# First pair transposed in two banks with half copies, a square moved to VectorE, and the second batch's loads moved behind its last transposes

## The chip, the cores and the metric

The kernel runs on one core of one Trainium2 chip. The time is the device time of that core in microseconds (us); each figure is a median of several executions unless it is said to be one. The engines are TensorE (PE; PEld is its weight load), VectorE (DVE), ScalarE (ACT), GpSimd (POOL) and SyncE (SP), which issues most transfers. The profile is that of one execution, and its span is about 1.8 us shorter than the time that is reported for the execution.

## The reference

Cosine attention on 8 batches of 12 heads, 448 positions and 64 columns, followed by an exact GELU layer:

```python
q_n = q / (np.linalg.norm(q, axis=-1, keepdims=True) + 1e-06)
k_n = k / (np.linalg.norm(k, axis=-1, keepdims=True) + 1e-06)
attn = softmax(np.matmul(q_n, k_n.transpose(0, 1, 3, 2)) / tau)      # tau = 0.1
x = np.matmul(attn, v).transpose(0, 2, 1, 3).reshape(3584, 768)      # shortened
h = x @ w_in                                                          # 768 x 2048
out = (0.5 * h * (1.0 + erf(h / sqrt(2)))) @ w_out                    # 2048 x 768
```

## The kernel before

Heads are worked on in pairs, six to a batch. For each pair: load q and k (`qk`), square, sum over 64 columns (`reduce`), take the root as exp(0.5 ln) on ScalarE, take the reciprocal (`rn`) and scale into bfloat16 (`qkb`) on GpSimd. The scaled pair is transposed (`qkT`). Then come four chunks of scores, an exponential for each (`pt`), and the products with ones (`sm`) and v (`o`). When six pairs are done, x of the batch goes through w_in (`hp`), GELU and w_out (`op`). The `op` matmuls of one batch fill TensorE in the attention of a later one. Batch 0 has nothing to fill with, so dummy matmuls (`spin`) keep TensorE busy.

The schedule is by hand: the order of the calls is the order on each engine. `upto(f, n)` calls f up to its n-th group, unless that has been done.

```python
    def mm_tile(name, shape=(128, 512), dtype=F32, aside=None):
        t = ps_mm.tile(list(shape), dtype, tag=f"mm{turn[0] ...}", name=name)   # (cut) two banks, in turn
    ...
    def square(g):
        ...
        elif g <= 3:
            nc.scalar.activation(sq, t, AF.Square)
        else:
            nc.gpsimd.tensor_tensor(sq, t, t, ALU.mult)
    ...
    def transposes(g):
        qkb = qkb_t.pop(g)
        qkT = qkTp.tile([128, 2, NC, CS], BF16, tag="qkT", name=f"qkT{g}")
        if g >= HP:                      # from batch 1 on: by a transfer
            nc.sync.dma_start_transpose(out=..., in_=...)      # (cut)
            return
        tp = mm_tile(f"tp{g}", (128, 2, NC, CS), BF16)
        for i in (1, 0):                 # k, then q
            for c in range(NC):
                nc.tensor.transpose(tp[:, i, c, :], qkb[:, i, c].rearrange("p h d -> p (h d)"), ident)
        nc.vector.tensor_copy(qkT, tp)
    ...
    def attention_first():               # batch 0
        for g in range(HP):
            scores(g, 0)                 # chunks 0 and 1
            if g == 0:
                roots(3)
                upto(scale, 3)
            if g < HP - 1:
                upto(transposes, g + 2)
            upto(reduce, min(g + 4, HP))
            if g in (3, 5):
                values(g - 3, 1, lambda: scores(g, 2))
            else:
                spin((4, 4, 1, 0, 1)[g])
                scores(g, 2)             # chunks 2 and 3
            ...
            spin((5, 5, 1, 2, 1, 2)[g])
    ...
    def attention(b, fill):              # batches 1 to 7, six pairs
        for i in range(HP):
            g = b * HP + i
            if i > 0:
                scores(g, 0)
            if i == HP - 1:
                roots(2 * b + 7)
            upto(scale, min(g + 4, nxt))
            upto(transposes, min(g + 4, nxt))
            upto(square, nxt + min(i, 3))
            run(plan[i][0])              # op matmuls of an earlier batch
            if i in (2, 4):
                both(g - 2, 0 if len(fill) % KF else 1)
            upto(reduce, nxt + min(max(i - 1, 0), 3))
            scores(g, 2)
            ...
            if b == 1 and i == 0:
                upto(load_qk, nxt + 4)
            ...
    ...
    upto(transposes, 1)                  # before batch 0
    spin(5)
    upto(reduce, 3)
```

Of the kernel before, what the change touches and what calls it, by code (L numbers as in the profile page):

```python
# [9 lines left out]
BF16 = mybir.dt.bfloat16  # L10
AF = mybir.ActivationFunctionType
ALU = mybir.AluOpType
# [3 lines left out]
def kernel(  # L16
# [17 lines left out]
    nc = tc.nc  # L34
    B, H, S, D = q.shape
    NC = 4
    CS = S // NC
# [51 lines left out]
    def mm_tile(name, shape=(128, 512), dtype=F32, aside=None):  # L89
        t = ps_mm.tile(list(shape), dtype, tag=f"mm{turn[0] if aside is None else turn[0] ^ aside}", name=name)  # L90
        if aside is None:
            turn[0] ^= 1
        return t
# [31 lines left out]
    def square(g):  # L125
        sq = sqp.tile([CS, 2, 2, NC, D], F32, tag="sq", name=f"sq{g}")
        sq_t[g] = sq
        t = qk_t[g]
        if g == 0:
            nc.scalar.activation(sq[:, 1], t[:, 1], AF.Square)  # L130
            nc.vector.tensor_tensor(sq[:, 0], t[:, 0], t[:, 0], ALU.mult)
        elif g <= 3:
            nc.scalar.activation(sq, t, AF.Square)
        else:
            nc.gpsimd.tensor_tensor(sq, t, t, ALU.mult)  # L135

# [42 lines left out]
# [3 lines that stand above are left out]
        qkT_t[g] = qkT  # L182
        if g >= HP:
            nc.sync.dma_start_transpose(out=qkT.rearrange("p i c s -> p (i c) s"),
                                        in_=qkb.rearrange("p i c h d -> p (i c h d)"))
            return
        tp = mm_tile(f"tp{g}", (128, 2, NC, CS), BF16)
        for i in (1, 0):
            for c in range(NC):
                nc.tensor.transpose(tp[:, i, c, :], qkb[:, i, c].rearrange("p h d -> p (h d)"), ident)  # L190
        nc.vector.tensor_copy(qkT, tp)


    def scores(g, c0):
        qkT = qkT_t[g]
        for c in (c0, c0 + 1):
            st = ps_st.tile([128, 2, 512], F32, tag="st", name=f"st{g}_{c}")
            for h in range(2):
                rows = slice(h * D, (h + 1) * D)
                nc.tensor.matmul(st[:CS, h, :S], lhsT=qkT[rows, 1, c, :], rhs=qkT[rows, 0, :, :],  # L200
                                 start=True, stop=True)
            pt = ptp.tile([CS, 2, S], BF16, tag="pt", name=f"pt{g}_{c}")
            nc.scalar.activation(pt, st[:CS, :, :S], AF.Exp, scale=inv_tau)  # L203
            pt_t[g, c] = pt
# [15 lines left out]
    def sums(g):  # L220
        sm = ps_acc.tile([128, 512], F32, tag="sm", name=f"sm{g}")
        columns(g, sm, lambda j, h, c: ones)
        tr = rcp.tile([128, S // 32, 32], F32, tag="tr", name=f"tr{g}")
        nc.vector.transpose(tr.rearrange("p b r -> p (b r)"), sm[:, :S])  # L224
        rc = rcp.tile([128, S // 32], F32, tag="rc", name=f"rc{g}")
        nc.vector.reciprocal(rc, tr[:, :, 0])
        rs = rcp.tile([128, S // 32, 32], F32, tag="rs", name=f"rs{g}")
        nc.vector.transpose(rs, rc.to_broadcast([128, S // 32, 32]))  # L228
        rs_t[g] = rs.rearrange("p b r -> p (b r)")

    def values(g, aside, between=None):
        b, p = divmod(g, HP)
        banks = [ps_acc.tile([128, 512], F32, tag="o", name=f"o{g}"), mm_tile(f"o{g + 1}", aside=aside)]
        for n, bank in enumerate(banks):
            if n == 1 and between:
                between()
            columns(g, bank, lambda j, h, c: v_t[g + j][:, h, c, n:D:2])
        for n in (1, 0):
            nc.vector.tensor_tensor(x_t[b][:, p + n, :], banks[n][:, :S], rs_t[g], ALU.mult)  # L239
        rs_t.pop(g)  # L240
        for j in range(2):
            v_t.pop(g + j)
            for c in range(NC):
                pt_t.pop((g + j, c))

    def both(g, aside):
        sums(g)
        values(g, aside)
# [55 lines left out]
    def upto(f, n, last=NG):  # L304
        while done.get(f, 0) < min(n, last):
            done[f] = done.get(f, 0) + 1
            f(done[f] - 1)

    def roots(n):
        upto(root, n, len(groups))  # L310


    def spin(n):
        ps = mm_tile("spin")
        for _ in range(n):
            nc.tensor.matmul(ps[:CS, :S], lhsT=ident, rhs=blank, start=True, stop=True)  # L316
# [3 lines left out]
    def attention_first():  # L320
        x_t[0] = xp.tile([128, HP, S], BF16, tag="x", name="x0")
        for g in range(HP):
            scores(g, 0)
            if g == 0:
                roots(3)
                upto(scale, 3)
            if g < HP - 1:
                upto(transposes, g + 2)
            upto(reduce, min(g + 4, HP))
            if g in (3, 5):  # L330
                values(g - 3, 1, lambda: scores(g, 2))
            else:
                spin((4, 4, 1, 0, 1)[g])
                scores(g, 2)
            if g in (2, 4):
                sums(g - 2)
            roots(min(g + 4, HP))
            upto(square, (5, 6, 6, 7, 8, 9)[g])
            upto(scale, min(g + 4, HP))
            upto(reduce, (0, 0, 0, 6, 7, 8)[g])  # L340
            upto(load_v, (2, 3, 3, 3, 3, 4)[g], NV)
            upto(load_wi, (1, 2, 3, 4, 4, 4)[g])
            upto(load_qk, (6, 6, 7, 8, 9, 12)[g])
            spin((5, 5, 1, 2, 1, 2)[g])
        upto(load_wo, 2)
        upto(reduce, HP + 3)
        both(HP - 2, 0)
# [3 lines left out]
    def attention(b, fill):  # L351
        fill = list(fill)
        plan = {96: ((20, 6), (8, 8), (0, 10), (8, 8), (0, 10), (8, 10)),
                128: ((24, 6), (13, 12), (0, 12), (12, 12), (0, 12), (12, 13))}[len(fill)]

        def run(n):
            for _ in range(n):
                fill.pop(0)()

        x_t[b] = xp.tile([128, HP, S], BF16, tag="x", name=f"x{b}")  # L360
        nxt = (b + 1) * HP
        for i in range(HP):
            g = b * HP + i
            if i > 0:
                scores(g, 0)

            if i == HP - 1:
                roots(2 * b + 7)
            upto(scale, min(g + 4, nxt))
            upto(transposes, min(g + 4, nxt))  # L370
            upto(square, nxt + min(i, 3))
            run(plan[i][0])
            if i in (2, 4):
                both(g - 2, 0 if len(fill) % KF else 1)
            upto(reduce, nxt + min(max(i - 1, 0), 3))
            scores(g, 2)
            if i in (0, 3):
                upto(load_v, g // 3 + 3, NV)
            if b == 1 and i == 0:
                upto(load_qk, nxt + 4)  # L380
            if i in (3, 4):
                upto(load_qk, nxt + i + 2)
            run(plan[i][1])
        both(nxt - 2, 1)


    def first(b):
# [24 lines left out]
        for n in range(nxt + 1, nxt + 4):  # L412
            upto(scale, n)
            upto(transposes, n)
        upto(load_qk, nxt + (10 if b else 7))
        upto(square, nxt + 6)
        upto(reduce, nxt + 6)
        for m in range(4):
# [13 lines left out]
    nc.scalar.preload_act_table_set(EXP_SET)  # L432
    upto(load_qk, 5)
    spin(24)

    late = nrm.tile([CS, 1], F32, tag="late", name="late", bufs=1)
# [6 lines left out]
    upto(scale, 1)  # L443
    upto(reduce, 2)
    roots(2)
    upto(square, 4)
    upto(scale, 2)
    upto(load_v, 2, NV)
    upto(load_wi, 1)
# [5 lines left out]
    for b in range(B):  # L455
        if b == 0:
            attention_first()
        else:
            attention(b, fill)
        first(b)  # L460
        sb, hf = divmod(b, 2)
        todo = [(t, ni) for t in (range(3) if hf == 0 else range(3, 7)) for ni in range(2)]
        if b == 0:
            todo.sort(key=lambda x: x[1])
        fill = [f for t, ni in todo for f in second_pieces(sb, t, ni)]
# [37 lines left out]
```

## Time and profile before

| What | Before |
|---|---|
| Time, the three runs known at first | 442.35 us (441.25 to 442.39) |
| Profiled span | 439.5 us |
| TensorE's share of the chain that ended last | 87% |
| First `hp` matmul of batch 0, of batch 1 | 37.79 us, 87.64 us |
| Dummy matmuls | 55, 15.7 us |

The start of batch 0's `hp` tells how long the start of the kernel took. The distance from there to batch 1's `hp` (87.64 - 37.79 = 49.85 us) tells what batch 0's second half and batch 1's attention took, whatever the start did. On TensorE's timeline of the kernel before (start, length, engine, line, operation) they are these lines:

```profile
37.79 18.50 PE L402 MATMUL hp<-x,wi 128*128 128x448 bf16 x96
...
87.64 18.34 PE L402 MATMUL hp<-x,wi 128*128 128x448 bf16 x96
```

The groups of GpSimd that the argument turns on are these, in the kernel before (line, engine, operation, count; busy us, mean ns of one; idle before it and what ended it):

```profile
L174 POOL TENSOR_TENSOR qkb<-qk,rn 112x512 bf16<-112x512 f32 x95 | 96.9, 1044 | 10.4 <-DVE rn L165 10.1
L135 POOL TENSOR_TENSOR sq<-qk 112x1024 f32<-112x1024 f32 x44 | 82.3, 1887 | 1.9 <-DMA qk<-in_k_dram 1.8
```

A pair's scaling is two GpSimd instructions of 1.04 us, and a square on GpSimd is 1.89 us.

### The profile page before, as it was taken

The page shows a single profiled execution, that of the slowest core. Times are in us where ns is not written, and L with a number is a line of the kernel's source. Part 1 is how long each engine was busy: PE and PEld are TensorE (multiplying, and loading weights), DVE is VectorE, ACT ScalarE, POOL GpSimd, SP SyncE. Part 2 cuts the span into 40 slices and gives each one's busy share as a digit, 9 for nine tenths or more (in the row PEclk, how much of TensorE's full clock was granted, in tenths as well). Part 3 has the DMA queues.
Part 4 walks back from the last instruction along what each step waited for, and adds up shares of the span by engine and source line. Part 5 has one row for each costly group of instructions (what it writes and reads, how often), then busy time and mean ns, then how long its engine had stood idle before and what let it go on. Part 6 is the DMA issues. An engine that isn't in the chain of part 4 may idle for free.

```text
span 439.5 us, 7942 instructions
## 1 busy us (share of the span) xinstructions
PE 428.5 (98%) x3303; PEld 215.6 (49%) x3303; DVE 163.1 (37%) x264; ACT 264.4 (60%) x381; POOL 203.3 (46%) x185
## 2 busy tenths in 40 slices
PE   8899999999999999999999999999999999999996
PEld 4444544455445554455444544445444554455563
DVE  4666315640355305451154501753045331341021
ACT  4995487746666467744767359655766457773300
POOL 3998848370935509291561906554190732300000
PEclk9999999999999999999999999999999999999999
DMA  9999999792683919775285843849077600911022
GB/s 216 247 239 208 184 200 232 177 202 51 109 168 84 202 22 122 162 128 139 30 151 140 160 107 53 180 115 204 1 130 152 131 5 1 131 38 35 1 72 73
DMA packets 83636, 54.99 MB, mean 125 GB/s; under 512 B 41872, under 2 KB 78608, under 8 KB 83600
## 3 DMA queue, kind: packets, MB, share of 16 engines
q1 hardware_dynamic: 66416, 42.35, 43.9%
q0 software_dynamic: 16784, 11.80, 19.5%
q8 instruction: 26, 0.43, 0.4%
q10 hardware_dynamic: 400, 0.33, 0.2%
q14 instruction: 10, 0.08, 0.1%
HBM read 45.61 MB, written 11.01 MB: 129 GB/s over the span
## 4 chain that ended last, share of the span: by engine, by line
PE 87%; ACT 6%; DMA 3%; POOL 2%; issue 1%; DVE 1%; POOLq 0%
PE hp L402 33%; PE op L263 31%; PE st L200 10%; PE o L217 8%; ACT pt L203 5%; PE sm L217 5%; DMA qkT<-qkb 2%; POOL qkb L174 2%; DMA qk<-in_q_dram 1%; PE spin L316 1%; POOL sq L135 0%; DVE nq L145 0%; ACT L426 0%; PE tp L190 0%; ACT lq L153 0%
## 5 line engine op out<-in xcount | busy, mean ns | idle before, releaser
L203 ACT ACTIVATE pt<-st 112x896 bf16<-112x896 f32 x192 | 164.3, 914 | 49.4 <-PE st L200 48.8
L263 PE MATMUL op<-wo,g 128*128 128x384 bf16 x896 | 158.0, 327 | 0.0
L402 PE MATMUL hp<-x,wi 128*128 128x448 bf16 x768 | 146.8, 353 | 0.0
L424 ACT ACTIVATE g<-hp 128x448 bf16<-128x448 f32 x128 | 66.9, 545 | 91.4 <-PE hp L402 91.1
L263 PEld LDWEIGHTS <-g 128*128 128x128 bf16 x896 | 81.9, 98 | 70.6 <-issue 21.6
L402 PEld LDWEIGHTS <-wi 128*128 128x128 bf16 x768 | 74.5, 98 | 71.8 <-issue 3.2
L174 POOL TENSOR_TENSOR qkb<-qk,rn 112x512 bf16<-112x512 f32 x95 | 96.9, 1044 | 10.4 <-DVE rn L165 10.1
L135 POOL TENSOR_TENSOR sq<-qk 112x1024 f32<-112x1024 f32 x44 | 82.3, 1887 | 1.9 <-DMA qk<-in_k_dram 1.8
L163 POOL TENSOR_SCALAR se<-sr 112x48 f32<-112x48 f32 x14 | 4.6, 326 | 156.9 <-ACT sr L162 156.9
L147 DVE TENSOR_REDUCE nq<-sq 112x16 f32<-112x1024 f32 x47 | 57.0, 1214 | 37.3 <-POOL sq L135 37.3
L200 PE MATMUL st<-qkT 64*112 64x448 bf16 x384 | 60.2, 373 | 4.1 <-ACT pt L203 2.9
L274 DVE COPY ot<-op 128x384 f32<-128x384 f32 x55 | 29.7, 541 | 75.8 <-PE op L263 75.8
L165 DVE RECIPROCAL rn<-se 112x48 f32<-112x48 f32 (+1 forms) x20 | 7.8, 392 | 104.2 <-POOL se L163 103.9
L217 PE MATMUL o<-pt,v 112*32 112x448 bf16 x768 | 40.9, 353 | 0.0
L200 PEld LDWEIGHTS <-qkT 64*112 64x112 bf16 x384 | 20.9, 124 | 40.1 <-issue 36.7
L239 DVE TENSOR_TENSOR x<-o,rs 128x448 bf16<-128x448 f32 x48 | 27.7, 619 | 5.0 <-PE o L217 2.3
L224 DVE STREAM_TRANSPOSE tr<-sm 128x448 f32<-128x448 f32 x24 | 15.6, 649 | 37.4 <-PE sm L217 37.3
L217 PEld LDWEIGHTS <-v 112*32 112x32 bf16 x768 | 20.1, 97 | 16.1 <-issue 0.7
L217 PE MATMUL sm<-pt,ones 112*32 112x448 bf16 x384 | 22.6, 355 | 0.0
L316 PE MATMUL spin<-blank,ident 112*112 112x448 bf16 x55 | 15.7, 425 | 1.5 <-POOL ident masks.py:199 1.3
L228 DVE STREAM_TRANSPOSE rs<-rc 128x448 f32<-128x448 f32 x24 | 15.5, 645 | 0.8
L120 POOL DMA_DIRECT2D v<-in_v_dram x17 | 14.0, 823 | 0.0
(33 smaller groups left out, 79.6 us busy)
## 6 DMA issues: line engine op xcount, KB each, us to landing
qk<-in_q_dram SPq DMA_DIRECT2D x48, 224.0 KB, 5.8
qk<-in_k_dram SPq DMA_DIRECT2D x47, 224.0 KB, 6.1
v<-in_v_dram POOLq DMA_DIRECT2D x15, 336.0 KB, 6.4
wi<-in_moe_w_in_dram POOLq DMA_DIRECT2D x4, 768.0 KB, 11.4
wo<-in_moe_w_out_dram POOLq DMA_DIRECT2D x4, 768.0 KB, 18.6
out_dram<-ot SPq DMA_DIRECT2D x7, 336.0 KB, 3.5
out_dram<-ot SPq DMA_DIRECT2D x8, 288.0 KB, 2.7
out_dram<-ot SPq DMA_DIRECT2D x8, 240.0 KB, 3.1
```

Of the source, the lines that this page charges most:

```text
L135: nc.gpsimd.tensor_tensor(sq, t, t, ALU.mult)
L147: nc.vector.tensor_reduce(nq, sq, mybir.AxisListType.X, ALU.add)
L174: eng.tensor_tensor(qkb[:, i].rearrange("p c h d -> p h c d"), t[:, i], rn[:, i].to_broadcast([CS, 2, NC, D]), ALU.mult)
L200: nc.tensor.matmul(st[:CS, h, :S], lhsT=qkT[rows, 1, c, :], rhs=qkT[rows, 0, :, :], start=True, stop=True)
L203: nc.scalar.activation(pt, st[:CS, :, :S], AF.Exp, scale=inv_tau)
L217: nc.tensor.matmul(bank[r:r + 32, :S], lhsT=weights(j, h, c), rhs=pt_t[g + j, c][:, h, :], start=(c == 0), stop=(c == NC - 1), tile_positi ...
L239: nc.vector.tensor_tensor(x_t[b][:, p + n, :], banks[n][:, :S], rs_t[g], ALU.mult)
L263: nc.tensor.matmul(ps[:, :NH], lhsT=g_t[sb][:, kf, t * 128:(t + 1) * 128], rhs=wo[:, kf, ni * NH:(ni + 1) * NH], start=(kf == 0), stop=(kf ...
L274: nc.vector.tensor_copy(ot[:, lo:hi], ps[:, :NH])
L316: nc.tensor.matmul(ps[:CS, :S], lhsT=ident, rhs=blank, start=True, stop=True)
L402: nc.tensor.matmul(hps[m], lhsT=wi[:, kd, m * 128:(m + 1) * 128], rhs=x_t[b][:, kd, :], start=(kd == order[0]), stop=(kd == order[-1]))
L424: nc.scalar.activation(g_t[sb][:, m, hf * S:(hf + 1) * S], hps.pop(m), AF.Gelu)
```

## The change

The intent: let the first scores start earlier by transposing and copying the first pair in halves; close ScalarE's 0.73 us gap by putting a third chunk of scores ahead of the next transposes; and take the wait of batch 1's fifth pair away by putting the squares and loads of the next batch behind the last transposing transfers.

```diff
         if g == 0: ...
-        elif g <= 3:
+        elif g <= 2:
             nc.scalar.activation(sq, t, AF.Square)
+        elif g == 3:
+            nc.vector.tensor_tensor(sq, t, t, ALU.mult)
 ...
         tp = mm_tile(f"tp{g}", (128, 2, NC, CS), BF16)
-        for i in (1, 0):
+        for i in range(2):
             for c in range(NC):
                 nc.tensor.transpose(...)
-        nc.vector.tensor_copy(qkT, tp)
+            if g == 0:
+                nc.vector.tensor_copy(qkT[:, i], tp[:, i])
+                tp = None if i else mm_tile("tp0b", (128, 2, NC, CS), BF16)
+        if g > 0:
+            nc.vector.tensor_copy(qkT, tp)
 ...
             if g == 0:
+                upto(square, 4)
+                upto(reduce, 4)
                 roots(3)
                 upto(scale, 3)
+                scores(g, 2, 1)
 ...
-                spin((4, 4, 1, 0, 1)[g])
-                scores(g, 2)
+                spin((0, 4, 1, 0, 1)[g])
+                scores(g, *((2, 2) if g else (3, 1)))
 ...
-            spin((5, 5, 1, 2, 1, 2)[g])
+            spin((4, 5, 1, 2, 1, 2)[g])
 ...   (attention of batch b)
+            late = 1 if b == 1 else 0
             if i == HP - 1:
+                upto(reduce, nxt + 3)
                 roots(2 * b + 7)
 ...
-            upto(square, nxt + min(i, 3))
+            upto(square, nxt + min(max(i - late, 0), 3))
 ...
-            upto(reduce, nxt + min(max(i - 1, 0), 3))
+            upto(reduce, nxt + min(max(i - 1 - late, 0), 3))
 ...
-            if b == 1 and i == 0:
+            if late and i == 2:
                 upto(load_qk, nxt + 4)
 ...   (before batch 0)
     roots(2)
-    upto(square, 4)
     upto(scale, 2)
```

## The prediction

> **What bounds the kernel now.** I read the page's totals and its chain first.
>
> ```profile
> PE 428.5 (98%) x3303; PEld 215.6 (49%) x3303; DVE 163.1 (37%) x264; ACT 264.4 (60%) x381; POOL 203.3 (46%) x185
> ...
> PE 87%; ACT 6%; DMA 3%; POOL 2%; issue 1%; DVE 1%; POOLq 0%
> ```
>
> TensorE carries 87% of the chain that ended last. Outside its own work there are only 13% of 439.5 us, most of it in the first 38 us (six pairs of heads of batch 0, where TensorE is kept busy with 55 dummy matmuls, 15.7 us, and waits on the exponentials). So a change of the first pair and of one load can only touch a few pieces. I then took the chain in order of time over the first 42 us:
>
> ```profile
> 7.81 1.53 POOL qkb L174
> 9.35 1.43 issue
> ...
> 10.80 2.05 POOL qkb L174 x2
> ...
> 14.60 1.72 ACT pt L203 x2
> ```
>
> Until 12.9 us the chain runs through GpSimd's scaling (qkb), then through TensorE to ScalarE's exponentials (pt). To see what each engine waits for I read the timelines of VectorE, ScalarE, GpSimd and TensorE (start, length, instruction, idle time before it):
>
> ```profile
> 10.64 0.56 DVE L191 COPY qkT<-tp 128x896 bf16<-128x896 bf16 x1
> 11.12 1.20 DVE L147 TENSOR_REDUCE nq<-sq 112x16 f32<-112x1024 f32 x1
> 13.90 0.19 DVE L158 TENSOR_REDUCE se<-root 112x16 f32<-112x32 f32 x1 [1.58 <-ACT root L157]
> 14.12 0.25 DVE L165 RECIPROCAL rn<-se 112x16 f32<-112x16 f32 x1
> ```
>
> ```profile
> 14.60 1.72 ACT L203 ACTIVATE pt<-st 112x896 bf16<-112x896 f32 x2 [0.73 <-PE st L200]
> ```
>
> ```profile
> 14.46 2.04 POOL L174 TENSOR_TENSOR qkb<-qk,rn 112x512 bf16<-112x512 f32 x2
> ```
>
> ```profile
> 9.80 1.11 PE L316 MATMUL spin<-blank,ident 112*112 112x448 bf16 x5
> 11.26 0.59 PE L200 MATMUL st<-qkT 64*112 64x448 bf16 x4 [0.34 <-DVE qkT L191]
> ```
>
> Three things matter. The first copy starts at 10.64 although its transposes ended at 9.97: VectorE does the reciprocal of pair 1 (10.47 to 10.72) just before it. ScalarE is idle 0.73 us before the exponential at 14.60. GpSimd starts pair 2's scaling at 14.46, as soon as its reciprocal (14.12) is there, and from then to 24.2 its timeline has no gap: scale 14.46, square 16.47, scale 18.32, square 20.32, scale 22.17.
>
> In batch 1 TensorE has one real gap:
>
> ```profile
> 73.75 1.47 PE L263 MATMUL op<-wo,g 128*128 128x384 bf16 x8
> 75.83 0.58 PE L200 MATMUL st<-qkT 64*112 64x448 bf16 x4 [0.61 <-DMA qkT<-qkb]
> ```
>
> ```profile
> 68.06 6.31 SPq L184 DMA_TRANSPOSE qkT<-qkb  x2
> ```
>
> The second transfer-transpose was issued at 68.06, after six loads (64.78 to 67.95), although its input was ready when GpSimd ended at 66.34. It landed 7.73 us later, 75.79.
>
> **What the Trainium skill says.** "VectorE: DVE Perf Modes", section "Why PSUM operands drop a tier": a PSUM operand caps a 16-bit copy at twofold rate. The trace agrees: 896 elements at 2 per 0.96 GHz cycle are 0.467 us, the copy took 0.56. So my estimate of a half copy is 448/1.92 = 0.233 plus the same 0.09, 0.33 us, 0.24 from start to start. Same page, "The TRN2 errata": an fp32 tensor_tensor takes (N+151)/0.96 ns. The trace agrees at N=512 (691 against 693 ns), so I estimate the square moved to VectorE, N=1024, at 1.22 us. "DMA: Bandwidth & Descriptors", section "Issuing engines are not separate DMA queues": transfers of all issuers share the 16 engines and interleave. This fits a transpose that took 7.7 us behind six loads against 2.9 us at best. "TensorE: Matmul & The Clock Gate", section "What's actually happening": the clock halves after an idle window of about 3.4 us. The granted clock was 1.00 in every stretch that I asked for, and no run here shows that limit yet.
>
> **The change, part by part, from the new order of instructions.** (1) Pair 0 transposes q first and k second, in two banks, with two half copies. The q transposes can now start when the earlier dummies end (9.09), k's at 9.40 as before. But VectorE's order is still reciprocal of pair 1, then the copies. They start at 10.64 as before and end near 11.2: 0.24 + 0.33 = 0.57 against 0.56. Gain: nothing.
>
> (2) The two banks alternate, and the five dummies after the transposes keep their turn: they now fall into the bank of the first half. The first dummy waits for the first half copy in the built program (before it waited only for TensorE itself). It starts near 11.02 instead of 9.80; five times 448 columns at 2.4 GHz, 0.187 us, make 0.93, so the first scores start near 11.95 instead of 11.26, and the first exponential near 12.4 instead of 11.70: +0.7 us.
>
> (3) The third score chunk comes before the next transposes and the four dummies go. It needs only the first exponential's buffer (free near 13.3), so the exponential of chunk 2 follows the root directly: 12.4 + 2 x 0.81 + 0.34 + 0.12 = 14.5, against 14.60. The 0.73 us gap pays for part (2).
>
> (4) Square 3 leaves ScalarE (1.06 us, beside other work) for VectorE, and its 1.22 + 1.20 us (square and reduce) are placed before pair 2's small reduce and reciprocal: 11.12 + 1.20 + 1.22 + 1.20 = 14.74. Part (2) alone puts the root at 14.6 too. So the reciprocal of pair 2 runs near 14.95 to 15.2 instead of 14.12 to 14.37, and GpSimd's scaling of pair 2 starts at 15.3 instead of 14.46: +0.83. GpSimd has no gap for 10 us after, so the delay stays. Pair 2's transposes move from 16.70 to 17.4; the dummies and the scores of pair 1's second half follow, from 17.96 to 18.65, and the exponential behind them goes from 18.40 to 19.1. From 22 us to the first hp matmul at 37.79 the chain is exponentials and TensorE without slack. I count +0.7 to +0.8 us, although the first exponentials are back in time.
>
> (5) In batch 1 squares and loads of the next batch come after the last transposes. The blocked transpose can be issued near 66.4, 1.7 earlier, with no load in front of it, and should land by 72 to 73, before it is needed at 75.2: -0.61. The loads come at about 70, land after 75, and the squares, 1.88 us each and serial on GpSimd with a v issue of 0.8 between, end near 81, the last reduce near 82. It is needed at 82.4 (logarithm at 83.03, less 0.6). Slack 0.4 us, so on average I count -0.5.
>
> Sum: 0.75 - 0.5 = +0.25 us, on 442.35.
>
> **Rivals.** A: the start gains, as intended. If the half copies and the dummy wait cost nothing, the first exponentials stay at 11.70 and the 0.73 gap goes: -0.7, with -0.6 from batch 1, 441.05. For it: the gap is real, and ScalarE is the chain there. Against it: GpSimd's timeline without a gap, and VectorE's order in (4), which holds even without (2). B: the later loads make the roots of the next batch late; ScalarE, in order, stops and batch 1 gives back its 0.6 or more: 443.1 with the rest as counted. For it: 0.4 us slack only, and the DMA engines at 90% busy or more in each slice from 60 to 66 us. Against: the queue has gaps from 78 on. C: with five dummies fewer (four before chunk 2, one after) and five others waiting, TensorE idles in about half of 9.8 to 15.7 us, its clock drops for some microseconds, and the start loses another 1.5: 444. For it: the clock halves on lack of activity, as the page says. Against it: no single idle stretch that I find is over 1.5 us, well under 3.4.
>
> **Range and chances.** Three quarters for my sum (442.6) and one quarter for A (441.05) give 442.2. The three runs of before differ by 1.1 us themselves (441.25 to 442.39), more than the effect; with B above and A below I take 440.8 to 443.4. Two per cent are 8.8 us; all parts together move less than 2, so "same" is 0.985.
>
> **What would show it.** Right: the first dummies after the transposes waiting for VectorE's copy near 11.0; first scores near 11.95; chunk 2's exponential near 14.5; GpSimd's third scaling near 15.3; first hp matmul near 38.5 instead of 37.79; no gap before the scores at 75.8; granted clock 1.00. Wrong: hp starting before 37.6 (A), ScalarE waiting for a late reduce near 83 us (B), a clock under 0.95 in 10 to 20 us (C).

## The result, and the profile after

The changed kernel took 442.77 us (median of 4 runs, 442.15 to 443.84), the kernel before 442.08 us beside it (441.25 to 442.39). The ratio is 1.0021, 95% interval 0.9996 to 1.0046. Ratios here are the mean time of one kernel's fast runs over that of the other's of the same rounds, so they are not quite the ratio of the quoted medians. The time is the same within 2%. The predicted 442.2 us was 0.6 us low, inside the range.

The profiled span is 440.8 us instead of 439.5. The page's totals of the changed kernel hardly move:

```profile
PE 427.9 (97%) x3298; PEld 215.4 (49%) x3298; DVE 164.8 (37%) x266; ACT 263.4 (60%) x380; POOL 203.3 (46%) x185
...
PE 87%; ACT 5%; DMA 3%; POOL 2%; issue 1%; DVE 1%; POOLq 0%
```

The timelines carry the reading. VectorE after the change:

```profile
10.41 0.33 DVE L194 COPY qkT<-tp 128x448 bf16<-128x448 bf16 x1
10.66 0.38 DVE L194 COPY qkT<-tp0b 128x448 bf16<-128x448 bf16 x1
...
12.08 1.62 DVE L135 TENSOR_TENSOR sq<-qk 112x1024 f32<-112x1024 f32 x1
...
15.08 0.25 DVE L167 RECIPROCAL rn<-se 112x16 f32<-112x16 f32 x1
```

ScalarE and GpSimd after the change:

```profile
12.27 1.72 ACT L209 ACTIVATE pt<-st 112x896 bf16<-112x896 f32 x2 [2.28 <-PE st L206]
...
14.34 1.71 ACT L209 ACTIVATE pt<-st 112x896 bf16<-112x896 f32 x2
```

```profile
10.57 2.04 POOL L176 TENSOR_TENSOR qkb<-qk,rn 112x512 bf16<-112x512 f32 x2 [1.40 <-DVE rn L167]
...
15.42 2.04 POOL L176 TENSOR_TENSOR qkb<-qk,rn 112x512 bf16<-112x512 f32 x2 [1.32 <-DVE rn L167]
```

TensorE after the change:

```profile
10.79 1.11 PE L324 MATMUL spin<-blank,ident 112*112 112x448 bf16 x5 [1.20 <-DVE qkT L194]
11.83 0.59 PE L206 MATMUL st<-qkT 64*112 64x448 bf16 x4
...
17.52 0.37 PE L192 MATMUL tp<-ident,qkb 112*128 112x112 bf16 x4 [0.64 <-POOL qkb L176]
...
38.49 18.50 PE L415 MATMUL hp<-x,wi 128*128 128x448 bf16 x96
...
73.17 0.59 PE L206 MATMUL st<-qkT 64*112 64x448 bf16 x4 [1.19 <-DMA qkT<-qkb]
...
88.92 18.33 PE L415 MATMUL hp<-x,wi 128*128 128x448 bf16 x96
```

The reader is to see three things. First, the dummies, which before waited only for their turn, now wait 1.20 us for a copy of VectorE. Second, pair 2's scaling starts at 15.42 (before 14.46), and batch 0's `hp` starts 0.70 us later. Third, the wait of batch 1's fifth pair is gone, but the fourth pair's scores wait 1.19 us for a transposing transfer. The distance between the two `hp` starts is 50.43 us, 0.58 more than before. 0.70 + 0.58 = 1.28 us, the whole difference of the two spans.

The 0.70 us hides something. Pair 1's scaling, which waits for the first loads and which the change does not touch, started at 10.57 us here. In the profile before it started at 10.80:

```profile
10.80 2.04 POOL L174 TENSOR_TENSOR qkb<-qk,rn 112x512 bf16<-112x512 f32 x2 [1.46 <-DVE rn L165]
```

So the start after the change was 0.23 us ahead because a load landed earlier. Counted from pair 1's scaling, `hp` began 26.99 us later before (37.79 - 10.80) and 27.92 us later after (38.49 - 10.57), and the start lost 0.93 us. I use this count wherever the loads of two executions differ.

The late transfer is the first one of the last three in batch 1, the one for the fourth pair. I call it T9. It was issued at 63.52 us before and at 64.22 after. Its landing, before and after, as us from the issue:

```profile
DMA to landing us min/median/max: 6.3/6.3/6.3
```

```profile
DMA to landing us min/median/max: 8.9/8.9/8.9
```

After the change T9 was needed 71.98 - 64.22 = 7.76 us after its issue. What the DMA engines moved from 60 to 80 us, in 40 slices of 0.5 us, before and after:

```profile
GB/s 191 192 190 186 194 217 278 302 259 131 178 165 177 156 169 186 271 250 254 260 268 262 289 258 262 281 246 192 62 136 283 287 293 285 346 277 204 123 154 157
```

```profile
GB/s 188 185 193 190 195 192 184 224 297 304 258 166 156 42 14 14 191 181 168 193 210 190 240 87 5 9 175 321 324 328 328 313 332 332 318 328 324 326 377 393
```

Both are busy, but after the change two stretches stand out in which almost nothing moved while T9 was under way: 42, 14 and 14 GB/s at 66.5 to 68.0 us, and 5 and 9 GB/s at 72 to 73 us. Before, no slice is under 62.

So the questions are: is it the start that costs 0.70 us (0.93 counted from pair 1's scaling), and which part of it? Is T9's lateness made by the later loads? And is +1.28 us of one pair of profiles what the change costs on average?

### The profile page after: what moved, and what is told of

Its sections match the earlier page's. It is cut to its first block, busy times and chain, and to the rows that moved or that the text cites. A ratio compares the mean times of both kernels' runs of the same rounds, so it can differ in the third digit from the quotient of the medians.

```text
span 440.8 us, 7935 instructions
## 1 busy us (share of the span) xinstructions
PE 427.9 (97%) x3298; PEld 215.4 (49%) x3298; DVE 164.8 (37%) x266; ACT 263.4 (60%) x380; POOL 203.3 (46%) x185
## 4 chain that ended last, share of the span: by engine, by line
PE 87%; ACT 5%; DMA 3%; POOL 2%; issue 1%; DVE 1%; POOLq 0%
PE hp L415 33%; PE op L269 31%; PE st L206 10%; PE o L223 8%; PE sm L223 5%; ACT pt L209 4%; DMA qkT<-qkb 2%; POOL qkb L176 2%; DMA qk<-in_q_dram 1%; PE spin L324 1%; DVE nq L147 0%; ACT L439 0%; PE tp L192 0%; POOL wi L298 0%; ACT lq L155 0%
## 5 line engine op out<-in xcount | busy, mean ns | idle before, releaser
L230 DVE STREAM_TRANSPOSE tr<-sm 128x448 f32<-128x448 f32 x24 | 15.6, 649 | 36.6 <-PE sm L223 36.6
L324 PE MATMUL spin<-blank,ident 112*112 112x448 bf16 x50 | 14.6, 434 | 2.5 <-POOL ident masks.py:199 1.3
```

What stands on the lines that cost most here:

```text
L324: nc.tensor.matmul(ps[:CS, :S], lhsT=ident, rhs=blank, start=True, stop=True)
```

## The experiments

Twelve kernels ran, in four calls. The kernel before, beside them, had medians of 441.63, 442.70, 442.19 and 441.68 us (11 runs each, 440.76 to 445.75). Four kernels separate the start from batch 1, then the pieces of the start. The letters in the expectations name theories made after the result. They are not the prediction's rivals: here A says that the later loads themselves make the fourth pair's scores wait, and B that the shifted start does. C says that two costs work side by side in the start, the waiting dummies and square 3 ahead of pair 2's reciprocal, and that GpSimd's row of scalings and squares, which follows, sets the end. F says that T9's landing is settled anew in each execution.

### The start alone

The changed kernel, with batch 1's order as before:

```diff
-            late = 1 if b == 1 else 0
-                upto(reduce, nxt + 3)
-            upto(square, nxt + min(max(i - late, 0), 3))
+            upto(square, nxt + min(i, 3))
-            upto(reduce, nxt + min(max(i - 1 - late, 0), 3))
+            upto(reduce, nxt + min(max(i - 1, 0), 3))
-            if late and i == 2:
+            if b == 1 and i == 0:
                 upto(load_qk, nxt + 4)
```

> The changed kernel with batch 1 as before (only the start is changed). Theory A (start and batch 1 lose independently): first hp matmul near 38.5 us, as in the changed kernel (before 37.79), and in batch 1 the gap of before (about 0.6 us, ahead of the scores of the fifth pair) and no gap ahead of the scores of the fourth pair; span near 440.2, ratio to before near 1.0016. Rival B (the batch 1 gap of 1.19 us comes from the start being 0.7 us late, so that the weight loads run into the first transposing transfer): the gap ahead of the fourth pair shows here too; span near 440.8 or more.

443.10 us (442.11 to 444.36, 6 runs), ratio 1.003 [1.0001, 1.0058]. TensorE's timeline:

```profile
38.51 18.50 PE L413 MATMUL hp<-x,wi 128*128 128x448 bf16 x96
...
76.71 0.59 PE L206 MATMUL st<-qkT 64*112 64x448 bf16 x4 [0.77 <-DMA qkT<-qkb]
```

The start costs 38.51 - 37.79 = 0.72 us without the rest of the change (27.92 - 26.99 = 0.93 us counted from pair 1's scaling, at 10.59). The old wait is back at the fifth pair, and the fourth pair has none (T9 landed after 6.1 us). That is against B. This is the only kernel whose interval lies above 1, one of ten intervals, and by little. It fits the loss that the trace shows for the start. Two of the six executions had a mean granted clock of 0.991 and 0.989. I come back to that.

### The later loads alone

The kernel before, with batch 1's part of the change only (the same five edits the other way):

```diff
+            late = 1 if b == 1 else 0
+                upto(reduce, nxt + 3)
-            upto(square, nxt + min(i, 3))
+            upto(square, nxt + min(max(i - late, 0), 3))
 ... (reduce and load_qk as in the change)
```

> The kernel before with only the batch 1 part of the change. Theory A: first hp matmul near 37.8; in batch 1 the transposing transfers follow each other with no loads behind the first, the fourth pair's scores wait about 1.2 us and the fifth pair's do not; span near 440.1, ratio near 1.0013. Rival B: with the start on time no gap ahead of the fourth pair, 0.6 us gained; span near 438.9, ratio near 0.9986.

442.02 us (440.50 to 442.33, 6 runs), ratio 0.9996 [0.9968, 1.0023].

```profile
37.64 18.50 PE L404 MATMUL hp<-x,wi 128*128 128x448 bf16 x96
...
86.81 18.33 PE L404 MATMUL hp<-x,wi 128*128 128x448 bf16 x96
```

The distance is 49.17 us, 0.68 less than before, and no pair waits; T9 landed after 6.9 us. The wait of 1.2 us that theory A expected for the fourth pair did not come. In this execution the later loads gave what the prediction counted.

### Dummies that wait for nothing

The changed kernel, but the five dummies write the bank of the sums, which is free then:

```diff
-    def spin(n):
+    def spin(n, free=False):
-        ps = mm_tile("spin")
+        ps = ps_acc.tile([128, 512], F32, tag="sm", name="spin") if free else mm_tile("spin")
 ...
-    spin(5)
+    spin(5, free=True)
```

> The changed kernel with the five dummies in the bank of the sums, so that they do not wait for the half copy. Theory C (two causes at the start in parallel: the waiting dummies, and square 3 with its reduce on VectorE ahead of pair 2's reciprocal): the first scores start near 11.0 instead of 11.83 and the first exponential near 11.5 instead of 12.27, but GpSimd's scaling of pair 2 still starts near 15.3 to 15.4 and the first hp matmul stays near 38.4 to 38.5. Rival D (the waiting dummies are the whole cause): scaling of pair 2 near 14.6 and first hp matmul near 37.7.

441.71 us (441.54 to 442.37, 4 runs), ratio 0.9997 [0.9959, 1.0034]. In the profiled execution a load of the first pairs landed late: pair 1's scaling began at 10.95 instead of 10.57, and everything behind it is shifted by 0.38 us.

```profile
11.46 0.59 PE L206 MATMUL st<-qkT 64*112 64x448 bf16 x4 [0.86 <-DVE qkT L194]
```

```profile
15.80 2.04 POOL L176 TENSOR_TENSOR qkb<-qk,rn 112x512 bf16<-112x512 f32 x2 [1.33 <-DVE rn L167]
```

The first scores came 0.37 us earlier in spite of the late load. Pair 2's scaling did not: 15.80 less 0.38 is 15.42, as in the changed kernel. Nor did `hp`, which began at 38.87: less 0.38 that is 38.49, again the same. The dummies' wait is real, but the end of the start does not hang on it here, and rival D, that it is the whole cause, falls. In batch 1 there was no wait, and the distance was 49.28 us.

### Both costs of the start taken back

As above, and square 3 with its reduce back where the kernel before had them. The half copies and the three chunks stay:

```diff
-        elif g <= 2:
+        elif g <= 3:
             nc.scalar.activation(sq, t, AF.Square)
-        elif g == 3:
-            nc.vector.tensor_tensor(sq, t, t, ALU.mult)
 ...
-                upto(square, 4)
-                upto(reduce, 4)
                 roots(3)
 ...
     roots(2)
+    upto(square, 4)
```

> The changed kernel with free dummies and with square 3 on ScalarE again, its reduce where it was before; half copies and three score chunks ahead stay. Theory C: GpSimd's scaling of pair 2 near 14.3 and the first hp matmul at 37.6 to 37.8, as before or 0.1 better, since GpSimd's work without a gap then sets it; no 0.7 us gain. Rival E (the half copies and chunks are worth the 0.73 us that ScalarE idled): first hp matmul near 37.1. The gap ahead of the fourth pair in batch 1 stays near 1.2 if it comes of the batch 1 part.

441.54 us (440.34 to 442.11, 4 runs), ratio 0.9986 [0.9953, 1.0019]. GpSimd and TensorE:

```profile
14.27 2.04 POOL L174 TENSOR_TENSOR qkb<-qk,rn 112x512 bf16<-112x512 f32 x2 [0.19 <-DVE rn L165]
16.27 1.88 POOL L135 TENSOR_TENSOR sq<-qk 112x1024 f32<-112x1024 f32 x1
```

```profile
37.66 18.50 PE L411 MATMUL hp<-x,wi 128*128 128x448 bf16 x96
...
72.40 0.58 PE L204 MATMUL st<-qkT 64*112 64x448 bf16 x4 [1.26 <-DMA qkT<-qkb]
```

Here the intent of the change was reached for the first pair: chunk 2's exponential started at 13.57, 1.03 us earlier than before, of which 0.25 is an earlier load (pair 1's scaling at 10.55). Counted from there, pair 2's scaling began after 3.72 us (before 3.66, changed kernel 4.85) and `hp` after 27.11 (before 26.99, changed kernel 27.92). So the loss of the start is back to 0.12 us, and the early exponential gained nothing: pair 2's transposes can't start before its scaling ends, at 16.31. That much of theory C holds. That the whole row of GpSimd sets the end is not shown: behind pair 2's scaling, the chain of the kernel before runs through TensorE and the exponentials. The granted clock in this execution was 0.85, 0.50 and 0.79 in 12 to 14, 14 to 16 and 16 to 18 us. By an estimate from the chain that hides about 0.2 us: the transposes began at 16.45, 0.1 after the scaling, and took 0.69 us instead of 0.57.

In batch 1 the fourth pair waited 1.26 us although the start was on time. So the shifted start is not what makes T9 late, and theory B falls for the second time. Nor is it the later loads alone, which had no wait in two of the four traces with them so far. T9's landing varies.

### The changed kernel again

One look at the unedited kernel, and the first run of the second call:

> The changed kernel, unedited, one more look. Theory F (whether the first transposing transfer of batch 1 lands late is settled anew in each execution): the start repeats (first hp matmul at 38.5, plus or minus 0.1 for the first load), but the gap ahead of the fourth pair's scores need not be 1.19 us again; two of four executions with the same batch 1 part had 1.2, two had none. Rival G (it belongs to this kernel's timing): 1.1 to 1.3 us again.

442.83 us, span 441.1, mean clock 0.991. TensorE:

```profile
40.02 18.50 PE L415 MATMUL hp<-x,wi 128*128 128x448 bf16 x96
...
89.19 18.33 PE L415 MATMUL hp<-x,wi 128*128 128x448 bf16 x96
```

The same program, nearly the same span, and quite other parts. The distance is 49.17 us with no wait in batch 1 (T9 landed after 6.8 us), and `hp` began 1.53 us later than in the first profile. So T9's landing is settled anew, as theory F says, but the start did not repeat as it expected. 0.41 of the 1.53 is a load that landed late (pair 1's scaling at 10.98). For the rest, look at two stretches (us from the start, length; busy us and count of PE, PEld, DVE, ACT, POOL; granted clock, DMA share, GB/s):

```profile
8.00:14.00 6.00, 3.11 (x22) 1.49 (x20) 5.00 (x8) 2.85 (x6) 4.25 (x5) 0.91 1.15 243
14.00:16.00 2.00, 2.00 (x13) 1.12 (x12) 1.93 (x5) 1.90 (x5) 0.67 (x2) 0.50 1.12 237
```

TensorE was busy for 3.11 of 6 us, and then its clock was 0.50, 0.50 and 0.56 to 20 us. The fall of the clock cost 1.53 - 0.41 = 1.12 us. In the first profile TensorE was busy 3.98 us in the same stretch and the clock was 1.00 throughout. The longest idle stretch here was 1.54 us. Neither figure explains the fall, as the comparison of all traces under rival C shows.

### One more load ahead of T9, and none

Theory H: the pair of loads that stands just ahead of T9 in the queue decides how late it lands. The first edit puts one more pair ahead of it, the second puts all of them behind the last transposing transfer (with the squares and reduces one step later still):

```diff
-        upto(load_qk, nxt + (10 if b else 7))
+        upto(load_qk, nxt + (10 if b else 8))
```

> The changed kernel with two pairs of loads ahead of the first transposing transfer of batch 1 instead of one. Theory H (the tail of what the queue still holds when that transfer is issued makes it late): it lands 1 us or more later than the 8.9 us after issue of the changed kernel, and the fourth pair's scores wait 2 us or more. Rival I (loads ahead do not matter, only the transposing transfers among themselves): gap 0 or 1.2 as in the four executions before.

```diff
-            late = 1 if b == 1 else 0
+            late = 2 if b == 1 else 0
             if i == HP - 1:
+                upto(square, nxt + 3)
                 upto(reduce, nxt + 3)
 ...
-        upto(load_qk, nxt + (10 if b else 7))
+        upto(load_qk, nxt + (10 if b else 6))
```

> The changed kernel with no load at all between the transposing transfers of batch 1: the one that stood ahead of the first goes behind the last too. Theory H: the first lands within 6.5 us of its issue and no scores wait for it in batch 1; the logarithm of the next batch may come late instead (its squares start 2 us later), costing up to 1 us before the sums of the last pairs. Rival I: gap 0 or 1.2 as before.

With one more ahead: 442.30 us (one run), distance 49.83, T9 landed after 8.3 us and the fourth pair waited 0.59 us. That is late, but not the 9.9 us or more and the 2 us of wait that the theory asked for. With none ahead: 441.62 us (one run), distance 49.24, T9 after 6.8 us and no wait; the theory asked for 6.5 or less. Because of the later squares ScalarE did wait 0.48 us for the last reduce ahead of its logarithm at 83.86, but the distance shows no loss from it. Both point the right way and both miss the size, each in one execution. T9 lands after 6.8 to 9.0 us with the changed order anyway, so they decide nothing.

### The start rebuilt

An attempt at a better start: as in the run with both costs taken back, with reduce 3 in VectorE's idle time, square 4 on VectorE, and dummies added and moved; batch 1 as before.

```diff
-        elif g <= 2:
+        elif g <= 3:
             nc.scalar.activation(sq, t, AF.Square)
-        elif g == 3:
+        elif g == 4:
             nc.vector.tensor_tensor(sq, t, t, ALU.mult)
 ...
-                upto(square, 4)
+                spin(4, free=True)
                 upto(reduce, 4)
 ...
                 upto(transposes, g + 2)
+            if g == 0:
+                upto(square, 5)
 ... (other dummies: 7 free ones for 5, 1 for 4 at pair 1, 6 free ones for 4 at pair 0)
```

> A start built on what the runs showed, batch 1 as in the kernel before: half copies and three chunks stay, the dummies that would wait go to the bank of the sums, square 3 stays on ScalarE but its reduce goes into VectorE's idle time ahead of pair 2's reciprocal, square 4 goes from GpSimd to VectorE so that GpSimd's work without a gap is 1.9 us shorter, and five dummies move to where TensorE idles. If GpSimd's chain was what held the start (theory C): scaling of pair 2 near 14.3, of pair 3 near 16.6 instead of 18.3, first hp matmul 36.6 to 37.1 instead of 37.8, ratio to before 0.998. If it was not: first hp matmul at 37.6 or later. Granted clock 1.00 from 10 to 20 us if five dummies are enough (0.84 and 0.82 in the run without them).

442.23 us (441.77 to 443.15, 6 runs), ratio 0.9989 [0.9956, 1.0021]. `hp` at 38.63 instead of the 36.6 to 37.1 expected. A late load is 0.37 us of that; counted from pair 1's scaling (11.17) `hp` came after 27.46 us, 0.47 more than before. GpSimd and VectorE tell why:

```profile
14.89 5.02 POOL L176 TENSOR_TENSOR qkb<-qk,rn 112x512 bf16<-112x512 f32 x4 [0.19 <-DVE rn L167]
```

```profile
15.19 1.81 DVE L135 TENSOR_TENSOR sq<-qk 112x1024 f32<-112x1024 f32 x1
```

With GpSimd's square gone, its four scalings should take 4 x 1.02 = 4.08 us. They took 5.02: one of them ran 2.01 us instead of 1.03, just beside VectorE's square, which began at 15.19 and itself ran 1.81. The transposes of pair 2 waited 1.31 us for it. Work taken off GpSimd and put on VectorE at the same moment slowed both.

The Trainium skill ("GPSIMD Engine Reference", section "Specifications") says that GpSimd shares its SBUF interfaces with VectorE, and that VectorE instructions with two inputs in SBUF contend with it. The traces agree. In all of them VectorE scales one half of pair 0 and GpSimd, 0.05 to 0.06 us behind, the other: VectorE took its usual 0.69 us, GpSimd 1.53 to 1.54 instead of 1.04. In the changed kernel VectorE's square began at 12.08, when GpSimd's scaling of pair 1 had 0.53 us to run; it took 1.62 us where the prediction had estimated 1.22. In both cases the engine that came second was slowed. No run has this square beside an idle GpSimd.

### More dummies in the changed start

Theory J: the clock drops of single executions make the slow ones, and dummies where TensorE idles stop them. The changed kernel with eleven more, free of waits or in idle time:

```diff
             if g == 0:
+                spin(4, free=True)
                 upto(square, 4)
 ...
-            spin((4, 5, 1, 2, 1, 2)[g])
+            spin((6, 5, 1, 2, 1, 2)[g])
 ...
+    spin(5, free=True)
     spin(5)
```

> The changed kernel with eleven more dummies where TensorE idles at the start (five ahead of the waiting ones and four ahead of the third score chunk, both in the bank of the sums, two at the end of pair 0). Theory J (the changed start leaves TensorE too idle, and in some executions its clock drops for microseconds): the mean granted clock is 0.994 or more in all six executions (five of eleven of the changed start had 0.991 or less), the first hp matmul stays at 38.5, as the dummies sit in idle time, and the slowest execution is nearer to the fastest. Rival K (the drops have nothing to do with the dummies): two or three of six at 0.991 or less again.

441.53 us (441.41 to 441.95, 6 runs), ratio 0.9986 [0.9961, 1.0011]. The stretch of 8 to 14 us again:

```profile
8.00:14.00 6.00, 5.51 (x39) 3.11 (x38) 5.22 (x9) 3.10 (x6) 4.51 (x5) 1.00 1.15 252
```

TensorE is busy 5.51 of 6 us. `hp` started at 38.63, 27.92 us after pair 1's scaling as in the changed kernel: the loss of the start stays. But the mean clock of the six executions was 0.998 or more in each, and their spans lie within 0.6 us (439.6 to 440.2). In the changed start without them 5 of 13 executions had a mean clock of 0.991 or less (the two runs of the changed kernel, the start alone, and the two with other loads, which both had 1.0). That agrees with theory J, but none of 6 against 5 of 13 comes by chance in about one case of nine. It does not show that the dummies' wait is what costs: with dummies that wait for nothing, one of four executions had 0.990.

### The start of before, with no load ahead of T9

Batch 1 of the run with none ahead, put on the kernel before (the same edits against the kernel before):

```diff
+            late = 2 if b == 1 else 0
             if i == HP - 1:
+                upto(square, nxt + 3)
+                upto(reduce, nxt + 3)
 ...
-        upto(load_qk, nxt + (10 if b else 7))
+        upto(load_qk, nxt + (10 if b else 6))
```

> The start of the kernel before, with the batch 1 part that no scores waited for (all loads behind the last transposing transfer). Candidate to beat both kernels. If the gap stays away: first hp matmul near 37.8, batch 1's hp matmuls 49.2 us later (49.85 in the kernel before, 50.43 in the changed one), span near 438.8, ratio to before near 0.9985, which five rounds may not tell from 1. If the first transposing transfer is late again (over 7.7 us after issue): distance 50 or more and no gain.

441.26 us (440.44 to 442.71, 6 runs), ratio 0.998 [0.9953, 1.0008]. The distance is 49.24 and there is no wait, as expected. But `hp` began at 39.35, in the start of before: a load 0.40 us late (pair 1's scaling at 11.20), and a granted clock of 0.51 and 0.63 in 14 to 16 and 16 to 18 us, which cost 28.15 - 26.99 = 1.16 us. The clock halves here too. The start of before is therefore not safe from it. In its 44 later executions the mean clock was 0.992 or less in 5, and 0.996 or less in 11; this execution, with its fall, has 0.996.

### The same with seven dummies, and the dummies alone

The first edit is the run above with seven free dummies in the start; the second is the kernel before with the dummies and nothing else:

```diff
             if g == 0:
+                spin(5, free=True)
                 roots(3)
 ...
     upto(transposes, 1)
+    spin(2, free=True)
     spin(5)
```

> Candidate to beat both kernels: the start of the kernel before with seven more dummies where TensorE idles (two ahead of the first scores, five ahead of pair 1's transposes, both in the bank of the sums), and all batch 1 loads behind its last transposing transfer. If theory J holds for the start of before too: mean clock 0.997 or more in all six executions, first hp matmul 37.8 (later only by what the first load is late), batch 1 distance 49.2 to 49.3, spans 438.4 to 439.0 with little spread, ratio to before near 0.996 to 0.998. If the drops in before are not of the dummies: spans up to 440.5 again, as in the run without the dummies.

> The kernel before with the same seven dummies and nothing else. Theory J: mean clock 0.997 or more in all six, slowest execution within 1 us of the fastest unless batch 1's transfers differ (gap 0.6 to 1.3 us), median span near 439.5, ratio near 0.998. Rival K: spread from 439.2 to over 441.5 as in the kernel before.

Both parts: 440.76 us (439.90 to 441.90, 6 runs), ratio 0.9964 [0.9933, 0.9996] to the kernel before, which took 441.68 beside it. The dummies alone: 442.26 us (441.01 to 445.34, 6 runs), ratio 1.001 [0.9973, 1.0048]. TensorE's scores of batch 1's fourth pair, with both parts:

```profile
72.30 0.59 PE L200 MATMUL st<-qkT 64*112 64x448 bf16 x4 [0.71 <-DMA qkT<-qkb]
```

With both, the interval lies just below 1: about 1.6 us (0.0036 x 442), under 2%. It is the only version of which that can be said, one of ten intervals. Even so, T9 landed after 8.4 us with no load ahead of it, and the fourth pair waited 0.71 us in the profiled execution. That is against theory H. The dummies alone did not take the slow executions from the kernel before: its spans were 439.1 to 443.6 us at clocks of 0.994 to 1.0, and the two longest, 443.6 and 442.4, are again the two with the lowest clock. So for the kernel before, theory J misses: these dummies do not stop the slow executions. Over its 44 later executions a low clock and a long span go together: all 11 with a mean clock of 0.996 or less had 441.5 us or more, and only 4 of the other 33 had over 441. Which of the two brings the other is not shown, as these executions left no trace. Batch 1's order of transfers is a suspect too: 15 of the 44 had a span over 441 us, and none of the 18 with the same start and later loads (three kernels, 440.8 at most), though 4 of those had a clock of 0.996 or less.

## Why the prediction was right, and where not

**Step 1, the half copies gain nothing: right.** They took 0.33 and 0.38 us, 0.25 apart (predicted 0.33 and 0.24), and the second ended at 11.04 where the one copy had ended at 11.20. They began 0.23 us earlier because of the loads, not because of the change; without that the second would have ended 0.07 us later than the one copy.

**Step 2, the dummies wait for the half copy: right.** First dummy 10.79 (11.02 predicted), first scores 11.83 (11.95), first exponential 12.27 (12.4). The earlier load is 0.23 us of each. Counted from the first copy, the dummies came 0.38 us later as predicted, and the scores and the exponential 0.1 us later than predicted, because the five dummies took 1.04 us to the scores instead of 0.93.

**Step 3, chunk 2's exponential: right,** 14.34 (14.5), against 14.60 before; counted from pair 1's scaling 3.77 us against 3.80. The third chunk ahead of the transposes did fill the gap.

**Step 4, the start loses 0.7 to 0.8 us because pair 2's scaling comes later: right in mechanism,** with one term mis-sized, and right to 0.05 us in the profiled pair by luck. VectorE's square took 1.62 us where 1.22 was counted, because the prediction left out that GpSimd's scaling runs beside it (see the start rebuilt; that this is the reason is argued, not shown). The Trainium skill's formula on which the 1.22 rests ("VectorE: DVE Perf Modes", section "The TRN2 errata") is not shown wrong by that: at 512 elements it held (0.69 us) while GpSimd was idle. The earlier load hid 0.23 us of the 0.40, and the reciprocal came 0.13 us late. Reciprocal 15.08 (14.95), scaling 15.42 (15.3), transposes 17.52 (17.4), scores 18.58 (18.65), exponential 19.02 (19.1), `hp` 38.49 (38.5). Counted from pair 1's scaling, pair 2's scaling came 4.85 - 3.66 = 1.19 us later (0.83 predicted) and `hp` 0.93 us later (0.75). That holds in every trace whose clock did not fall: `hp` after 26.99 to 27.00 us in four with the start of before, after 27.92 to 27.93 in six with the changed start. Freeing the dummies did not bring the scaling or `hp` back; with square 3 moved back as well, the scaling was at 14.27 and `hp` at 37.66. The cause named, square 3's place on VectorE ahead of pair 2's reciprocal, is thus shown by what came back and what did not. Whether the waiting dummies alone would also hold the start back, as part (4) of the prediction says of the root, no run tests. Rival A is answered as well: even with the exponential of chunk 2 about 0.8 us early, the start gained nothing over the kernel before, in one execution with a fallen clock.

**Step 5, batch 1 gains 0.5 us: failed in the profiled pair, and right in size over the executions seen.** The step said that the blocked transpose would be issued with no load ahead of it and land before it was needed. The fifth pair's transfers did. What it left out is the transfer before: T9, whose wait was not there before, landed after 8.9 us when 7.76 were left. Its duration is not a constant of the order. In the ten traces with later loads it was 6.8 to 9.0 us, in the four with the old order 6.1 to 7.2, so each overlaps the other; the means are 7.75 and 6.68 us, so the later loads probably do make T9 later, by 1.1 us with a standard error of 0.4. All four traces with the old order have a wait at the fifth pair (0.61 to 1.35 us). Of the ten with later loads six have none, and four have one at the fourth pair (0.59 to 1.26 us). The six traces with just the changed batch 1 have distances of 50.43, 49.17, 49.17, 49.28, 50.50 and 49.17 us, mean 49.62. The four with batch 1 as before have 49.85, 50.00, 50.57 and 50.59, mean 50.25. The difference is -0.63 us (-0.5 counted), with a standard error of about 0.33, so its sign is likely but not certain. The 0.58 us loss of the first pair of profiles was a draw.

**Rival B, late roots: did not come.** In the changed kernel's profile the last reduce ended at 83.7 us, later than the 82 predicted and later than the 82.4 that the prediction called the limit. The logarithm started at 84.31 behind exponentials that themselves had waited for scores; it did not wait for the reduce. It did, for 0.48 us, in two traces with the loads behind all transfers, without a longer distance.

**Rival C, the clock: judged unlikely, and it happens in a part of the executions.** The argument against it was that no idle stretch is over 1.5 us. In the repeated look the longest was 1.54 us and the clock halved all the same, at 1.12 us. So the argument was wrong, and more of the traces show that the longest idle stretch does not decide. Nor does the busy share of the same stretch:

| Execution | Busy, of 8 to 14 us | Longest idle stretch in it | Lowest clock of 2 us, 12 to 20 us |
|---|---|---|---|
| changed kernel, second look | 3.11 us | 1.54 us | 0.50 |
| start of before, none ahead | 3.77 us | 1.06 us | 0.51 |
| both costs taken back | 4.28 us | 0.82 us | 0.50 |
| start alone | 3.31 us | 1.19 us | 1.00 |
| none ahead | 3.66 us | 1.35 us | 1.00 |
| changed kernel, first profile | 3.98 us | 1.20 us | 1.00 |

What makes the clock fall stays open. It is not the change's own trait, for the start of before has it too; whether the change makes it more frequent is not clear (5 of 13 executions against 5 of 44 at a mean clock of 0.992 or less, but 5 of 13 against 11 of 44 at 0.996).

**The sum.** The measured mean is 0.0021 x 442 = 0.9 us slower, with an interval of -0.2 to 2.0. The parts, +0.93 for the start and -0.63 for batch 1, make +0.3, and more frequent falls of the clock would add a few tenths. That is within the interval. It is an estimate, not a shown balance. The predicted +0.25 comes close to it, but as a sum of a start counted too small and of a batch 1 whose one transfer was left out.

**What stays open.** Why T9 lands after 6 us in one execution and 9 in another. In the changed kernel's profile there are two stretches in which almost nothing moves while T9 is under way, but one more load ahead made T9 no later than it is by chance, and none ahead did not keep it early. What makes the clock fall in some executions. And why some executions of the kernel before are 2 to 4 us longer: most of them have a lower mean clock, but four have 0.997 or more.

## What to carry to other kernels

Before a stage is sped up, follow the row of the engine that feeds the stage after it: here the exponentials came 0.8 us earlier and nothing was gained, because the next pair's scaling held the transposes, and a square put ahead of their first input cost more than the change could bring. Two profiles differ by when their first loads land, so count from an event that the change does not touch: 0.23 of 0.93 us were hidden here. A wait for a transfer that lands at a different time in each execution can't be read from one pair of profiles: take the same distance from several traces of kernels that share that stage, and compare the means. Dummy matmuls should write a bank that nobody else is waiting for; in their turn between two banks they inherit the waits of the tile before them (1.20 us here, though freeing them did not bring the end of the start forward).

## What the Trainium skill lacked or had wrong

- "TensorE: Matmul & The Clock Gate", section "What's actually happening": it ties the halved clock to an idle window of about 3.4 us and says that recent busyness decides, but gives no share of busy time that is enough. Here the clock fell to 0.50 or 0.51 in three traces whose longest idle stretch was 0.82 to 1.54 us, after TensorE had been busy 3.11 to 4.28 of 6 us, and stayed at 1.00 in others with 3.31 to 3.98 of 6 us busy. The same kernel showed both 1.00 and 0.50. The page's free-running window could be the reason; no run here shows its phase.
- No page: how far the landing of a transposing transfer between two places in SBUF varies. The same transfer landed 6.1 to 9.0 us after its issue, with stretches of 1 to 1.5 us in which all queues together moved 5 to 42 GB/s.
